# Reordered first steps of a fused FFT-mixing and ELU kernel: one weight load earlier, three reads behind the A writes, X units a step later

## The chip, the cores and the metric

The kernel runs on one core of a Trainium2 chip. The metric is the device time of one execution in microseconds (us); it was taken in three runs, and a fourth execution was recorded by the profiler. The engines are TensorE (PE for matmuls, PEld for weight loads), VectorE (DVE), ScalarE (ACT), GpSimd (POOL) and SyncE (SP), which here only issues DMA transfers. SyncE's transfers go through the DMA queue q1, GpSimd's through q0. Each engine works through its own instructions in program order; a semaphore holds an instruction back until what it reads is there.

## The reference

The input `x` has 8 batches of 3008 tokens of 256 channels. Each batch goes through a Fourier transform along its tokens, a complex linear layer with soft threshold, and the inverse transform. The result goes through two dense layers with an ELU between.

```python
X = np.fft.rfft(x, axis=1)
Yr = Xr @ w_r - Xi @ w_i + b_r
Yi = Xr @ w_i + Xi @ w_r + b_i
Yr = np.sign(Yr) * np.maximum(np.abs(Yr) - 0.01, 0.0)
Yi = np.sign(Yi) * np.maximum(np.abs(Yi) - 0.01, 0.0)
y = np.fft.irfft(Yr + 1j * Yi, n=x.shape[1], axis=1)
h = y @ moe_w_in                     # 256 -> 2048
g = np.where(h > 0.0, h, np.exp(np.minimum(h, 0.0)) - 1.0)
return g @ moe_w_out                 # 2048 -> 256
```

## The kernel before

**Two parts that run interleaved.** The transform of a batch is a chain of units, each a few matmuls with an evacuation from PSUM: six units A (first factor of the forward transform, `unit_A`), eight X (second factor, `unit_X`), twelve M (the complex layer, `unit_M`), six B (first factor of the inverse, `unit_B`) and eight Y (second factor, `unit_Y`). Between A and X, and between B and Y, the data change their layout by way of DRAM: A units write to `DA`, `load_Z` reads it back as `Z` (two pieces, rows 0 to 7 and 8 to 31 of its second axis); B units write to `DB`, and four `load_Bs` read it back as `Bs` 0 to 3. X units 0 and 1 read the first piece of Z, units 2 to 7 the second. Y units 2w and 2w+1 read `Bs` w and fill a quarter of `yT`, the input of the dense layers. `load_x` brings x of a batch in three transfers of 1 MB, on GpSimd's queue.

**Steps.** The dense layers are cut into 376 steps, 47 for each batch: step i takes a block of 512 tokens and two of the sixteen slices of 128 hidden channels. It has four matmuls into PSUM (`front_mm`, L790), exponentials on ScalarE (L804, L808), a clamp (`least`: VectorE for the first four steps, L815, then GpSimd, L813), a mix on VectorE (`mix`, L825) that gives `gT`, and two steps later eight matmuls with `w_out` (`back`, L845). Every eighth step the block's result is copied to `osb` and written to the output by four transfers (L856, L863).

**The plan.** `plan(b)` lays out what runs beside the steps of batch b: the rest of that batch's Y units and the whole chain X, M, B and the first two Y of batch b+1, and the A units of batch b+2. It makes a list `seq` with one unit for a step. `lead` is the step of the first entry, `early` says how many Y units come ahead of X, `fill` holds units that may stand among the M and B units, and `cut` says behind which M unit each of them goes (-1: ahead of the first M). `due` is the step at which the next batch's Y unit 0 stands. `f0[t]` holds the unit that is emitted between step t's two pairs of matmuls, `f1[t]` what is emitted behind them: loads, sums of weights (`weight_sum`, on GpSimd), scalings. In a step with an M unit the clamp is done by ScalarE in another form; GpSimd does four operations for each M (L274, L275, L240, L278).

**The first batch.** The transform of batch 0, the A units of batch 1 and Y units 0 and 1 of batch 0 run ahead of step 0. `w_in` is loaded in quarters on SyncE's queue (`load_w_in`) and scaled into `w_in_s` (`scale_w_in`); the last quarter's two scalings stand in steps 3 and 4 (L735), and steps 6 and 7 are the first that read it. `w_out` is loaded in halves on GpSimd's queue (`load_w_out`, L660). `gate(src)` is a copy of one element by GpSimd (L665), which waits until the transfer that brings `src` has landed; what GpSimd issues behind it starts later. There are three: ahead of x of batch 1, ahead of w_out's second half (on `Bs` 2), and in step 3 ahead of x of batch 2 (on the second piece of `Z` of batch 1).

**The order around the change.** For batch 0 `seq` is y2 to y5 in steps 1 to 4, X0 to X7 in 5 to 12, y6 in 13, M and B units from 14 on (M0, M1, M2, M3, B0, M4, M5, B1 and so on to B4 in 30), y7 in 31, B5 in 32, A0 to A3 in 33 to 36, the next batch's y0 and y1 in 37 and 38, A4 and A5 in 39 and 40. x of batch 2 is asked for in steps 3, 8 and 13. The tokens of batch 1 enter in step 40, for which its y0 and y1 are needed. Step 33 has the output writes of a block.

Of the kernel before, what the change touches and what calls it, by code (L numbers as in the profile page):

```python
# [25 lines left out]
def kernel(  # L26
# [73 lines left out]
    Z_of = {}  # L100
# [4 lines left out]
    Bs_of = {}  # L105
    yT_of = {}
    def load_x(b, ci, m0=0, m1=8):

        src = bass.AP(
            tensor=x.tensor,  # L110
            offset=x.offset + (b * S + 8 * ci + m0) * D,
            ap=[[N1 * D, N2], [(NJ - 1) * D, 2], [D, m1 - m0], [1, D]],
        )
        dst = xts[ci][:, m0:m1, :]
        nc.gpsimd.dma_start(dst, src.bitcast(F32R))
# [25 lines left out]
    def unit_A(b, u, alone=False, on_dve=False, ahead=False):  # L141
        ci, uu = u // 2, u % 2
        if uu == 0:
            if ahead and ci == 1:
                A_of[b, ci] = xtp.tile([P, 3, 8, D], BF16, name="A", tag="XT")[:, 0]
            elif ahead and ci == 2:
                A_of[b, ci] = late2.tile([P, 8, D], BF16, name="A", tag="osb")
            elif alone:
                A_of[b, ci] = wk4.tile([P, 8, D], BF16, name="A", tag="Bs")
            else:  # L150
                A_of[b, ci] = wk2.tile([P, 8, D], BF16, name="A", tag="A")
            if ci == 0:
                DA_of[b] = dram.tile([NJ, P, D], BF16, name="DA", tag="DA")
        xt, A = xts[ci], A_of[b, ci]
        dav = DA_of[b].rearrange("j p d -> p j d")
        ps = unit_ps("aps", alone or ahead)
        for j in range(2):
            nc.tensor.matmul(  # L158
                ps[:, j, :], lhsT=M1[:],
                rhs=xt[:, 4 * uu + 2 * j : 4 * uu + 2 * j + 2, :], start=True, stop=True,  # L160
            )
        def done():
            evac(
                A[:, 4 * uu : 4 * uu + 4, :].rearrange("p n d -> p (n d)"),
                ps[:].rearrange("p a b -> p (a b)"), on_dve,
            )
            j0 = 8 * ci
            if alone:
                j0 += 4 * uu
                nc.sync.dma_start(dav[:, j0 : j0 + 4, :], A[:, 4 * uu : 4 * uu + 4, :])  # L170
            elif uu == 1:
                nc.sync.dma_start(dav[:, j0 : j0 + 8, :], A[:])

        later(alone or ahead, done)
# [165 lines left out]
    def load_Bs(b, w):  # L340

        Bs = wk4.tile([4 * K1, 8, D], BF16, name="Bs", tag="Bs")
        dv = DB_of[b].rearrange("k (c h m) d -> (k c h) m d", c=2, h=2)
        nc.sync.dma_start(Bs[:], dv[:, 8 * w : 8 * w + 8, :])
        Bs_of[b, w] = Bs
# [22 lines left out]
    def idle_pe(n):  # L368

        for _ in range(n):  # L370
            nc.tensor.matmul(ips[:], lhsT=busy[:, 0:P], rhs=busy[:], start=True, stop=True)
# [278 lines left out]
    def load_w_in(q):  # L650
        if q < 3:
            wf = late3.tile([P, 2, FQ], F32, name="w_in_f", tag="Et")
        else:
            wf = late2.tile([P, 2, FQ], F32, name="w_in_f", tag="osb")
        nc.sync.dma_start(wf[:], w_in_v[:, :, q * FQ : q * FQ + FQ])
        w_in_f.append(wf)

    def load_w_out(hh):
        hf = slice(hh * NFT // 2, (hh + 1) * NFT // 2)
        nc.gpsimd.dma_start(w_out_r[:, hf, :], w_out_v[:, hf, :])  # L660

    def gate(src):

        t = gatep.tile([P, 1], F32, name="gate", tag="gate")
        nc.gpsimd.tensor_copy(t[0 : src.shape[0], :], src)  # L665
# [7 lines left out]
    for ci in range(3):  # L673
        load_x(1, ci)
    load_w_out(0)
    nc.vector.tensor_scalar(w3[:], v3[:], CMAGIC, -CMAGIC, ALU.add, ALU.add)
    nc.vector.tensor_tensor(w3[:], v3[:], w3[:], ALU.subtract)
    nc.scalar.copy(bias_p[:], brow[:])
# [53 lines left out]
    def scale_w_in(q, on_dve, c=slice(0, 2)):  # L732
        dst = w_in_s[:, c, q * FQ : q * FQ + FQ]
        if on_dve:
            nc.vector.tensor_scalar_mul(dst, w_in_f[q][:, c], 2.0 / S)  # L735
        else:
            nc.scalar.activation(dst, w_in_f[q][:, c], AF.Copy, scale=2.0 / S)

    scale_w_in(0, True)
    for u in range(6):  # L740
        unit_A(1, u, on_dve=bool(u % 2), ahead=True)
        if u == 1:
            scale_w_in(1, True)
            for w in (2, 3):
                load_Bs(0, w)
            gate(Bs_of[0, 2][:, 0, 0:1])
            load_w_out(1)
            load_w_in(3)
        idle_pe(2)
    scale_w_in(2, False)  # L750
    for s0, s1 in ((0, 8), (8, NS)):
        load_Z(1, s0, s1)
# [116 lines left out]
    def put(kind, b, *a):  # L869
        return ({"A": unit_A, "X": unit_X, "M": unit_M, "B": unit_B, "Y": unit_Y}[kind], (b, *a))  # L870

    def plan(b):

        f0 = [[] for _ in range(PER)]
        f1 = [[] for _ in range(PER)]
        n1, n2 = b + 1, b + 2
        lead = int(b == 0)
        early = 6 if b == 0 else 4
        seq = [("y", u) for u in range(2, early)]
        rest_ = []  # L880
        if n1 < B:
            due = 37 + b
            seq += [("X", u) for u in range(8)]
            fill = [("y", u) for u in range(early, 8)]
            if n2 < B:
                fill += [("A", u) for u in range(6)]
            else:
                fill += [("-",)] * 6
            room = max(0, min(10, due - 5 - (b > 0) - lead - len(seq) - 17))
            fill, rest_ = fill[:room], fill[room:]  # L890
            cut = [-1, 11, 0, 4, 8, 2, 6, 10, 1, 11][: len(fill)]
            fill = fill[::-1]
            seq += [fill.pop() for c in cut if c < 0]
            for k in range(12):
                seq.append(("M", k // 2, k % 2))
                if k % 2 and k > 1:
                    seq.append(("B", k // 2 - 1))
                for c in cut:
                    if c == k:
                        seq.append(fill.pop())  # L900
            seq.append(("B", 5))
            k = due - lead - len(seq)
            seq += rest_[:k] + [("-",)] * (k - len(rest_))
            seq += [("n", 0), ("n", 1)] + rest_[k:]
        else:
            seq += [("y", u) for u in range(early, 8)]
        xs = (3, 8, 13) if b == 0 else (1, 4, 7)
        for t, u in enumerate(seq, lead):
            if u[0] == "y":
                f0[t].append(put("Y", b, u[1]))  # L910
            elif u[0] == "n":
                f0[t].append(put("Y", n1, u[1]))
            elif u[0] == "A":
                if n2 < B:
                    f0[t].append(put("A", n2, u[1]))
            elif u[0] == "M":
                f0[t].append((unit_M, (n1, *u[1:])))
            elif u[0] != "-":
                f0[t].append(put(u[0], n1, *u[1:]))
            if u == ("X", 7):  # L920
                for k in range(2):
                    f1[t + 1].append((unit_D, (n1, k)))
            if u == ("B", 5):
                f1[t + (0 if b == 0 else 1)] += [(load_Bs, (n1, w)) for w in range(4)]
            if u == ("A", 5) and n2 < B:
                f1[t] += [(load_Z, (n2, s0, s1)) for s0, s1 in ((0, 8), (8, NS))]
        if b == 0:
            f1[5].append((weight_sum, (0,)))
            f1[6].append((weight_sum, (1,)))
            f1[7].append((weight_sum, (2,)))  # L930
            f1[3].append((scale_w_in, (3, True, 0)))
            f1[4].append((scale_w_in, (3, True, 1)))
            f1[xs[0]].append((lambda: gate(Z_of[1][:, 16, 0:1]), ()))
        if n2 < B:
            for ci in range(3):
                f1[xs[ci]].append((load_x, (n2, ci)))
        return f0, f1
# [5 lines left out]
    for i in range(n + LAG):  # L943
        split = False
        if i < n:
            r = i % PER
            if r == 0:
                f0, f1 = plan(i // PER)
                used = [bool(u0 or u1) for u0, u1 in zip(f0, f1)]
                kinds = ["M" if any(f is unit_M for f, a in f0[k]) else "F" for k in range(PER)]  # L950
# [76 lines left out]
```

## Time and profile before

| what | value |
|---|---|
| three runs | 904.35, 905.66, 907.62 us, median 905.66 |
| the profiled execution | 905.97 us |
| its span, from first to last instruction | 904.2 us |
| PE busy | 873.7 us (97%) |
| ACT busy | 709.6 us (78%) |
| POOL busy | 664.8 us (74%) |
| DVE busy | 654.7 us (72%) |
| chain of waits, shares | PE 84%, POOL 6%, issue 4%, DVE 3%, DMA 2% |
| DMA moved | 106.32 MB, mean 118 GB/s |

How to read the rows. A timeline row has start, duration, engine, line, operation, tile written and tile read, shapes and a count; merged rows cover several instructions. In square brackets stands how long the engine was idle ahead of it and what ended the idle time. The row of 40 digits is the engine's busy share in 40 slices of 22.6 us, in tenths. A row of a stage (two times with a colon) has the stage's length, the busy time and count of PE, PEld, DVE, ACT and POOL, the granted clock of TensorE as a share of full speed, the busy share of the DMA engines (it can pass 1, as transfers overlap), and the GB/s moved. Rows with SPq are SyncE's issues of transfers, not the transfers themselves; rows with POOL and DMA_DIRECT2D are GpSimd's.

### The profile page before, as it was taken

The numbers are of one execution on the slowest core, as the hardware profiler recorded it, in microseconds if no ns is written. First come the engines' busy times: TensorE is split into PE (matmuls) and PEld (weight loads), VectorE is DVE, ScalarE is ACT, GpSimd is POOL, SyncE is SP. The second block draws the span as 40 slices with busy tenths as digits, with TensorE's granted clock in tenths as the row PEclk, the third lists the DMA queues.
The fourth block names the chain that finished last, engine by engine and source line by source line (L and its number), as shares of the span: only waits on it lengthen the run. The fifth ranks groups of instructions, "written<-read, shape, count | busy, mean of one in ns | idle before, by whom it ended". The sixth has DMA issues, their size and how long they took to land.

```text
span 904.2 us, 18246 instructions
## 1 busy us (share of the span) xinstructions
PE 873.7 (97%) x6778; PEld 668.6 (74%) x6889; DVE 654.7 (72%) x1066; ACT 709.6 (78%) x1132; POOL 664.8 (74%) x998
## 2 busy tenths in 40 slices
PE   8885999999999999999999999999999999999997
PEld 3444767887778777787778877788777877778776
DVE  8772777668867687667777687767876677777775
ACT  6673888788887888888887888878887888777664
POOL 6704797669966799568986699767986589866664
PEclk9996999999999999999999999999999999999999
DMA  8995314651265411761138502573136211141011
GB/s 264 319 261 141 103 57 118 198 168 43 71 188 141 140 47 51 218 182 66 47 103 225 164 24 71 148 202 117 50 98 172 79 42 53 48 117 48 25 47 47
DMA packets 90677, 106.32 MB, mean 118 GB/s; under 512 B 5270, under 2 KB 81308, under 8 KB 87228
## 3 DMA queue, kind: packets, MB, share of 16 engines
q1 hardware_dynamic: 84332, 77.62, 30.6%
q0 software_dynamic: 5968, 27.26, 9.4%
q8 instruction: 54, 0.88, 0.4%
q14 instruction: 35, 0.29, 0.1%
q10 hardware_dynamic: 288, 0.26, 0.1%
HBM read 55.32 MB, written 49.81 MB: 116 GB/s over the span
## 4 chain that ended last, share of the span: by engine, by line
PE 84%; POOL 6%; issue 4%; DVE 3%; DMA 2%; ACT 1%; SPq 0%; ACTq 0%; DVEq 0%; POOLq 0%
PE ps_o L845 36%; PE hps L790 32%; PE mps L256 5%; PE bps L314 3%; PE xps L192 2%; PE aps L158 2%; PE yps L355 2%; POOL Y L278 1%; PE mps L209 1%; POOL yb L274 1%; POOL Et L813 1%; POOL Xd L240 1%; POOL clip L275 1%; DMA Bs<-DB 1%; DMA xt<-in_x_dram 1%
## 5 line engine op out<-in xcount | busy, mean ns | idle before, releaser
L825 DVE SCALAR_TENSOR_TENSOR gT<-Et,hps 128x512 fp32r<-128x512 f32 x752 | 496.9, 684 | 193.6 <-POOL Et L813 168.7
L845 PE MATMUL ps_o<-w_out_r,gT 128*128 128x256 f32 x3008 | 478.9, 302 | 0.9 <-ACT osb L856 0.8
L813 POOL TENSOR_SCALAR Et<-Et 128x512 f32<-128x512 f32 x576 | 351.1, 617 | 166.7 <-ACT Et L808 165.7
L845 PEld LDWEIGHTS ps_o<-w_out_r,gT 128*128 128x128 f32 x3008 | 405.2, 189 | 52.9 <-ACT osb L856 4.4
L790 PE MATMUL hps<-yT,w_in_s 128*128 128x512 bf16 (+7 forms) x1622 | 418.6, 354 | 6.2 <-DVE gT L825 4.7
L808 ACT ACTIVATE Et<-hps 128x512 f32<-128x512 f32 x584 | 341.7, 603 | 103.3 <-PE hps L790 98.9
L790 PEld LDWEIGHTS <-w_in_s 128*128 128x128 bf16 x1728 | 118.9, 98 | 61.7 <-issue 26.0
L804 ACT ACTIVATE Et<-hps 128x512 f32<-128x512 f32 x168 | 100.6, 599 | 51.9 <-PE hps L790 46.8
L278 POOL TENSOR_TENSOR Y<-yb,clip 128x512 bf16<-128x512 f32 x84 | 108.4, 1290 | 0.3
L806 ACT ACTIVATE Et<-Et 128x1024 f32<-128x1024 f32 x84 | 89.0, 1059 | 2.7
L274 POOL TENSOR_TENSOR yb<-yb,bias_d 128x256 f32<-128x256 f32 x84 | 61.6, 734 | 13.3 <-DVE yb L266 12.4
L266 DVE TENSOR_TENSOR yb<-mps,Kb 128x512 f32<-128x512 f32 x84 | 58.1, 692 | 3.0
L275 POOL TENSOR_SCALAR clip<-yb 128x512 f32<-128x512 f32 x84 | 51.7, 615 | 7.4
L240 POOL TENSOR_TENSOR Xd<-XT 128x256 bf16<-128x256 bf16 x84 | 56.3, 673 | 0.0
L265 DVE TENSOR_TENSOR Kb<-mps,bias_bc 128x256 f32<-128x256 f32 x84 | 35.5, 423 | 27.9 <-PE mps L256 27.7
L126 ACT CAST XT<-xps 128x768 bf16<-128x768 f32 x61 | 48.5, 795 | 8.9 <-PE xps L192 8.9
L126 ACT CAST A<-aps 128x1024 bf16<-128x1024 f32 x45 | 45.4, 1011 | 7.3 <-PE aps L158 6.9
L256 PE MATMUL mps<-wsum,XT 128*128 128x256 bf16 x336 | 50.4, 273 | 0.0
L126 ACT CAST yT<-yps 128x752 bf16<-128x752 f32 x63 | 49.2, 780 | 1.4 <-PE yps L355 1.4
L328 ACT CAST Bz<-bps 128x1024 bf16<-128x1024 f32 x46 | 46.3, 1007 | 0.4 <-PE bps L314 0.4
L192 PEld LDWEIGHTS <-Z 96*128 96x128 bf16 x512 | 29.2, 99 | 22.5 <-DMA Z<-DA 7.4
L192 PE MATMUL xps<-M,Z 96*128 96x96 bf16 x512 | 33.0, 208 | 9.0 <-DMA Z<-DA 6.2
(117 smaller groups left out, 476.9 us busy)
## 6 DMA issues: line engine op xcount, KB each, us to landing
xt<-in_x_dram POOLq DMA_DIRECT2D x21, 1024.0 KB, 5.3
out_dram<-osb SPq DMA_DIRECT2D x158, 128.0 KB
Bs<-DB SPq DMA_DIRECT2D x32, 384.0 KB
DA<-A SPq DMA_DIRECT2D x21, 512.0 KB
DB<-Bz SPq DMA_DIRECT2D x21, 512.0 KB
Z<-DA SPq DMA_DIRECT2D x7, 1152.0 KB
Z<-DA SPq DMA_DIRECT2D x11, 384.0 KB
xt<-in_x_dram POOLq DMA_DIRECT2D x6, 512.0 KB, 5.9
```

The costliest lines, as they stand in the source:

```text
L126: nc.scalar.copy(dst, src)
L192: nc.tensor.matmul(psv[:, kk, 0 : 4 * K1], lhsT=Z[:, k, dt * P : dt * P + P], rhs=M2[:, k].rearrange("p c m -> p (c m)"), start=True, stop ...
L256: nc.tensor.matmul(dst, lhsT=lhs(dt), rhs=rhs(dt), start=dt == 0, stop=dt == 1)
L274: nc.gpsimd.tensor_tensor(yb[:, D : 2 * D], yb[:, D : 2 * D], bias_d[:], ALU.add)
L278: nc.gpsimd.tensor_tensor(Y_[:, i, :], yb[:], clips[0][:], ALU.subtract)
L790: nc.tensor.matmul(hps[s][:, c0:c1], lhsT=w_in_s[:, dt, ft * P : ft * P + P], rhs=yT_of[b][:, dt, t0 : t0 + c1 - c0], start=(dt == 0), sto ...
L804: nc.scalar.activation(e, h, AF.Relu, scale=-1.0)
L806: nc.scalar.activation(self.E, self.E, AF.Exp, scale=-1.0)
L808: nc.scalar.activation(e, h, AF.Exp)
L813: nc.gpsimd.tensor_scalar(e, e, 1.0, 0.0, ALU.min, ALU.max)
L825: nc.vector.scalar_tensor_tensor(g_of[self.i][:, p], self.E[:, p], -1.0, self.h[p], ALU.add, ALU.max)
L845: nc.tensor.matmul(po[q][:, i_ % 2, :], lhsT=gT[:, s, i_ * P : i_ * P + P], rhs=w_out_r[:, ft, :], start=(ft == 0 and i_ % 2 == 0), stop=( ...
```

## The change

Ahead of step 0, `load_w_out(1)` is called right behind `load_w_out(0)`; the small copy that stood ahead of it is gone. `load_Bs(0, 2)`, `load_Bs(0, 3)` and `load_w_in(3)` move from behind batch 1's second A unit to behind its sixth, so that on SyncE's queue the three A writes come ahead of them, and `load_Z` behind them as before.

In the plan of batch 0 an empty entry goes in behind y3, so that y4 and y5 stand in steps 4 and 5 and the X units in 6 to 13; y6 is in 14, and the M units begin in 15. y7 goes in behind M4 (step 21) and A0 ahead of B5 (33 and 34); A1 to A3 are in 35 to 37, the next y0 and y1 in 38 and 39, A4 and A5 in 40 and 41. The two scalings of w_in's last quarter are in steps 4 and 5, x of batch 2 is asked for in steps 14, 18 and 22, and the small copy on Z ahead of it is gone.

In the plans of the later batches `due` is one larger. So one more of `fill` goes in among the M and B units, and the next batch's y0 and y1 stand a step later, in steps 38+b and 39+b; the tokens that read them enter in step 40+b.

```diff
@@ -673,6 +673,7 @@
     for ci in range(3):
         load_x(1, ci)
     load_w_out(0)
+    load_w_out(1)
     nc.vector.tensor_scalar(w3[:], v3[:], CMAGIC, -CMAGIC, ALU.add, ALU.add)
@@ -741,12 +742,10 @@
         unit_A(1, u, on_dve=bool(u % 2), ahead=True)
         if u == 1:
             scale_w_in(1, True)
-            for w in (2, 3):
-                load_Bs(0, w)
-            gate(Bs_of[0, 2][:, 0, 0:1])
-            load_w_out(1)
-            load_w_in(3)
         idle_pe(2)
+    for w in (2, 3):
+        load_Bs(0, w)
+    load_w_in(3)
     scale_w_in(2, False)
     for s0, s1 in ((0, 8), (8, NS)):
         load_Z(1, s0, s1)
@@ -877,9 +876,11 @@
         seq = [("y", u) for u in range(2, early)]
+        if b == 0:
+            seq.insert(2, ("-",))
         rest_ = []
         if n1 < B:
-            due = 37 + b
+            due = 38 + b
@@ -888,7 +889,7 @@
-            cut = [-1, 11, 0, 4, 8, 2, 6, 10, 1, 11][: len(fill)]
+            cut = ([-1, 4] if b == 0 else [-1, 11, 0, 4, 8, 2, 6, 10, 1, 11])[: len(fill)]
@@ -898,13 +899,15 @@
+            if b == 0:
+                seq.append(rest_.pop(0))
             seq.append(("B", 5))
...
-        xs = (3, 8, 13) if b == 0 else (1, 4, 7)
+        xs = (14, 18, 22) if b == 0 else (1, 4, 7)
@@ -928,9 +931,8 @@
-            f1[3].append((scale_w_in, (3, True, 0)))
-            f1[4].append((scale_w_in, (3, True, 1)))
-            f1[xs[0]].append((lambda: gate(Z_of[1][:, 16, 0:1]), ()))
+            f1[4].append((scale_w_in, (3, True, 0)))
+            f1[5].append((scale_w_in, (3, True, 1)))
```

## The prediction

> **What bounds the kernel now.** I read the page first, then the list of waits, then the timeline of 60 to 100 us, then stages of the span and SyncE's queue. On the page TensorE is busy 97% of the span; behind the first slices the only dip, down to 5 tenths, is near 70 us, and every later slice but the last shows 9.
>
> ```profile
> PE   8885999999999999999999999999999999999997
> ```
>
> The long waits of the list all lie in that dip, and the timeline shows that they are one event.
>
> ```profile
> 66.51 0.61 PE L790 MATMUL hps<-yT,w_in_s 128*128 128x512 bf16 x2
> 73.03 0.82 PE L192 MATMUL xps<-M,Z 96*128 96x96 bf16 x8 [5.91 <-DMA Z<-DA]
> ...
> 77.79 0.18 POOL L665 CAST gate<-Z 96x1 f32<-96x1 bf16 x1 [16.74 <-DMA Z<-DA]
> 78.88 1.21 POOL L813 TENSOR_SCALAR Et<-Et 128x512 f32<-128x512 f32 x2
> 79.55 1.28 DVE L825 SCALAR_TENSOR_TENSOR gT<-Et,hps 128x512 fp32r<-128x512 f32 x2 [12.35 <-POOL Et L813]
> 80.29 1.01 PE L790 MATMUL hps<-yT,w_in_s 128*128 128x512 bf16 x2 [3.88 <-DVE gT L825]
> 86.68 0.60 PE L790 MATMUL hps<-yT,w_in_s 128*128 128x512 bf16 x2
> 88.82 0.61 PE L790 MATMUL hps<-yT,w_in_s 128*128 128x512 bf16 x2
> ```
>
> Step 5 begins at 66.51; its X unit waits 5.91 us for Z's first piece, until 73.03. GpSimd's small copy waits 16.74 us for the second piece, until 77.79; behind it in GpSimd's order stands step 4's clamp (L813), behind that VectorE's mix (L825), and behind that the PSUM bank that step 6 needs: 80.29. Step 8 begins at 86.68, step 9 at 88.82. An undisturbed X step is 88.82 - 86.68 = 2.14 us. Steps 5 to 7 took 86.68 - 66.51 = 20.17 us where three such take 6.42: **13.75 us** too long.
>
> ```profile
> 66.00:68.00 2.00, 1.12 (x8) 0.59 (x7) 1.20 (x3) 1.39 (x3) 0.00 (x0) 1.00 1.37 343
> 72.00:84.00 12.00, 7.09 (x37) 5.67 (x38) 2.57 (x4) 3.40 (x5) 5.86 (x9) 0.50 0.61 170
> ```
>
> In these stages (length, then busy time of PE, PEld, DVE, ACT, POOL, then granted clock, DMA share, GB/s) the clock is 1.00 ahead of the wait and 0.50 from 72 to 84. So of the 13.75 us, 5.91 and 3.88 are waits and the other 3.96 mostly work at half clock.
>
> **Why Z is late.** SyncE issues in this order; sizes are from the DMA view.
>
> ```profile
> 51.88 0.80 SPq L344 DMA_DIRECT2D Bs<-DB  x2
> ...
> 54.94 0.95 SPq L655 DMA_DIRECT2D w_in_f<-in_moe_w_in_dram  x1
> 55.99 1.94 SPq L172 DMA_DIRECT2D DA<-A  x2
> 69.17 0.79 SPq L181 DMA_DIRECT2D Z<-DA  x2
> ...
> Bs<-DB SPq DMA_DIRECT2D x4, 384.0 KB
> DA<-A SPq DMA_DIRECT2D x3, 512.0 KB
> Z<-DA SPq DMA_DIRECT2D x1, 1152.0 KB
> w_out_r<-in_moe_w_out_dram POOLq DMA_DIRECT2D x1, 1024.0 KB, 10.0
> w_in_f<-in_moe_w_in_dram SPq DMA_DIRECT2D x1, 512.0 KB
> Z<-DA SPq DMA_DIRECT2D x1, 384.0 KB
> ...
> 52.00:54.00 2.00, 2.00 (x10) 0.85 (x9) 1.18 (x2) 1.29 (x2) 0.00 (x0) 1.00 0.52 133
> 54.00:62.00 8.00, 6.06 (x55) 3.63 (x54) 5.51 (x9) 5.51 (x10) 1.10 (x2) 1.00 1.02 293
> 70.00:76.00 6.00, 2.97 (x18) 2.61 (x18) 0.00 (x0) 1.40 (x2) 0.00 (x0) 0.59 1.02 258
> ```
>
> The last two writes of A stand behind all four Bs (1.57 MB) and w_in (0.52 MB), and in their last stretch the 1.05 MB of w_out's second half runs beside them. The DMA engines are full (share 1.02). Z is issued when the last A write has landed, at 69.17.
>
> **The change, part by part.**
>
> (1) *Order on SyncE's queue, w_out out of the way.* The new order is Bs 0 and 1 (0.79 MB), three A writes (1.57), Bs 2 and 3 (0.79), w_in (0.52), Z (0.39 and 1.18). I let the queue move in order: 0.27 MB by 54.0 (2 us at 133 GB/s), then 293 GB/s. A has landed at 54.0 + (2.36 - 0.27)/0.293 = 61.1; Bs 2, 3 and w_in are through at 61.1 + 1.31/0.293 = 65.6; Z, at its own 258 GB/s, at 67.1 and 71.7. From the last byte to use I add 1.7 us: the old Z's 1.57 MB, at 258 from 70.0 on, ends at 76.1, and the copy that waits for it runs at 77.79. Usable: Bs 2 at 64.1, w_in at 67.3, Z at **68.8** and **73.4**. Needed: y4 stays in step 4, which begins a step ahead of 66.51, so 0.45 us later, at 64.8 (0.45 for the two matmuls ahead of a unit); X0 is now in step 6, at 66.51 + 2.14 + 0.45 = **69.1**, X2 two steps on at **73.4**. That leaves 0.7, 0.3 and 0.0 us. I take 0.3 us for the waits left; bounds are 0, and 3.4 by the first rival below. If the waits go, all 13.75 us go, since the half clock came with them.
>
> (2) *scale_w_in a step later.* The second scale now stands in step 5, directly ahead of step 6, whose matmuls read it.
>
> ```profile
> 66.78 0.42 DVE L735 TENSOR_SCALAR w_in_s<-w_in_f 128x512 bf16<-128x512 f32 x1
> ```
>
> The old one ended at 67.20, 0.69 us behind the front of the following step (66.51), which did not need it. The new one does the same a step later, and there it is needed: **+0.7 us**. With w_in usable at 67.3, 0.5 us behind the place of the new first scale (66.78), the bounds are 0 and 1.2.
>
> (3) *w_out's second half at 28 us.* It is issued in an idle gap of GpSimd's.
>
> ```profile
> 27.13 1.28 POOL L660 DMA_DIRECT2D w_out_r<-in_moe_w_out_dram  x1
> 32.92 1.24 POOL L300 TENSOR_SCALAR clip<-yb 128x512 f32<-128x512 f32 x1 [4.50 <-DVE yb L219]
> DMA to landing us min/median/max: 10.0/12.0/13.9
> 40.00:46.00 6.00, 5.95 (x44) 2.53 (x43) 3.41 (x5) 5.31 (x8) 4.19 (x6) 1.00 0.53 175
> ```
>
> The issue ends at about 29.7, ahead of the clip at 32.92: nothing. The first half landed at 27.13 + 13.9 = 41.0, so the second moves from 40 to 46, where 6 x 0.175 = 1.05 MB move now. At the 343 GB/s that w_out and SyncE's queue reached together (66 to 68 us), 2.06 MB would fit, 0.04 less than needed; at 293, 0.34 less. What is left over could delay the last DB write, and with it Bs 0, by 0.1 or 1.2 us; that write is issued only behind 49 us, so I take **+0.2**, bounds 0 and 1.2. *The Trainium skill, "DMA: Bandwidth & Descriptors", section "Queues, rings and completion order", speaks against this edit: a DMA engine goes round robin between the queues that have work, packet by packet, so w_out would take about half of each engine from the DB writes while both run. By that rule every DB write of this stage could end late by w_out's own 3.1 us (1.05 MB at 343 GB/s), but those issued ahead of 46 us have no reader before 51; the sum stays.*
>
> (4) *X units a step later, y7 among the M steps, x of batch 2 at steps 14, 18, 22, no small copies.* Steps and units stay in number, so TensorE's own time stays. What counts is GpSimd's work in the M steps of batch 0.
>
> ```profile
> 99.55 0.61 PE L790 MATMUL hps<-yT,w_in_s 128*128 128x512 bf16 x2
> 102.02 0.39 PE L790 MATMUL hps<-yT,w_in_s 128*128 128x512 bf16 x1
> 144.14 0.61 PE L790 MATMUL hps<-yT,w_in_s 128*128 128x512 bf16 x2
> 99.61 0.58 POOL L115 DMA_DIRECT2D xt<-in_x_dram  x1
> ```
>
> The 17 steps (12 M, 5 B) from 99.55 to 144.14 took 44.59 us; at the first one's 2.47 they would take 41.99, so 2.6 us are lost, to GpSimd, which the chain of waits follows through most of this stretch. The new order puts y7 among them, a step with 1.21 us of clamps in 2.14: 0.93 us relieved. Two x issues (0.58 each, steps 18 and 22) come in: 1.16. **+0.2 us**, bounds -0.9 and +1.2. The issue at 99.61 stood there before, too.
>
> (5) *y of batch 1 four steps behind that batch's last B, not five; step 33's four output writes now ahead of that B's write on SyncE.*
>
> ```profile
> 151.77 1.74 SPq L344 DMA_DIRECT2D Bs<-DB  x4
> 153.60 2.68 SPq L863 DMA_DIRECT2D out_dram<-osb  x4
> 158.38 0.50 PE L355 MATMUL yps<-M,Bs 96*128 96x94 bf16 x8
> 55.54 0.84 PE L355 MATMUL yps<-M,Bs 96*128 96x94 bf16 x16 [0.62 <-DMA Bs<-DB]
> ```
>
> From the first Bs issue to its use was 55.54 - 51.88 = 3.66 us, so here Bs was ready at 155.4 and needed at 158.4: 3.0 us in hand. One step less takes 2.1 to 2.5. The outputs' 2.68 us of issue begin as their block ends, and I estimate that 0.7 us of them stand ahead of the B write; their 0.52 MB may hold the rings for 1.8 us (at 293). So the wait lies between 0 and about 2: **+0.6 us**.
>
> (6) *Later batches: one more unit among the M steps, y of the next batch a step later.* The page's row shows TensorE at 9 tenths or more through all of them, so an M step is not shortened by what stands beside it: 0, bounds -0.5 and +0.5 as estimates from the 2.6 us of batch 0. The second y unit now ends in the step right ahead of its first reader.
>
> ```profile
> 269.71 0.78 ACT L126 CAST yT<-yps 128x752 bf16<-128x752 f32 x1
> 270.71 1.04 PE L790 MATMUL hps<-yT,w_in_s 128*128 128x512 bf16 x4
> ```
>
> Its cast ends at 270.49 and the next step begins at 270.71: covered, by 0.2 us.
>
> **Sum.** -13.75 + 0.3 + 0.7 + 0.2 + 0.2 + 0.6 = -11.75. The profiled execution took 905.97 us (span 904.2 and 1.8 around it), which becomes 894.2; it lies 0.3 above the median of the three runs, 905.66, which becomes **893.9**.
>
> **Rivals.**
>
> *Z is still late.* For it: three margins in (1) are 0.7 us or less. If the queue moves at Z's 258 GB/s throughout, and Bs and w_in share it with the A writes, A lands at 54.0 + 3.40/0.258 = 67.2; Z is issued 0.9 later and begins 0.9 behind that, as the old one did (69.17 to about 70), so it is usable at 72.2 and 76.8: 3.1 us of wait at X0 and 0.3 at X2, 3.1 more than taken: **897.0**. Against it: the queue moved 293 with both kinds on it. *By the Trainium skill, "TensorE: Matmul & The Clock Gate", part on the HAM clock gate, the clock halves behind an idle window of about 3.4 us; the trace agrees so far as a wait of 5.9 us was followed by 0.50. By that rule a wait of 3.1 just escapes it, and one of 3.5 costs up to 3.96 more, as here: 901.*
>
> *GpSimd becomes the bound at once.* Its three weight sums lay in the disturbed steps and cost nothing there; now they lie in X steps at full speed.
>
> ```profile
> 80.05 1.16 POOL L228 TENSOR_TENSOR wsum<-wcat_r 128x512 bf16<-128x512 bf16 x1
> ```
>
> If three of at most 1.16 us and the two x issues all come onto the path, it is 3.5 + 1.2 - 0.2 = 4.5 more: **898.4**. Against it: two clamps are 1.21 of a step's 2.14, so a sum fits but for 0.2.
>
> *Slower: GpSimd is held at the issue of w_out's second half.* No row shows five transfers of 1 MB in its queue at once. Were it held until the queue is empty, 41.0 + 3.1 = 44.1, the clip of 32.92 would be 11.2 us late, TensorE would idle behind it and go on at half clock for another 3.96 as above: +15.2, **909.1**. From a hold to about 41 us on (8.1 + 3.96 = 12.1), nothing of the gain is left. Against it: four went in one behind the other.
>
> *It does not do what it says*: A still lands near 69 us because something else than the order holds it. Then Z's wait stays, less the step that X has moved: near 903. No row speaks for it.
>
> **How the numbers follow.** The forecast holds 0.65; its own range, from the bounds taken together, is 891 to 896. Z still late 0.17, GpSimd 0.1, held 0.05, no effect 0.03. The range, 890.8 to 898.5, takes in the prices of the first two rivals. A change under 0.3%, 2.7 us, cannot be told from none: faster than 902.9 are the first three, 0.92; same 0.03; slower 0.05.
>
> **What would show it.** Right: no copy on Z in GpSimd's order, Z issued near 62, X0 at 69 to 70, clock 1.00 from 60 to 100. A scale of w_in that ends behind the front of step 6 shows (2); a wait of TensorE for Bs in step 38 shows (5); M steps of batch 0 that keep 2 to 3 us of loss show (4). Wrong would be a GpSimd issue of several us at 28, Z issued behind 66, or a clock below 1.00 after 60.

## The result and the profile after

| kernel | median | lowest to highest | runs | ratio to the kernel before, with its 95% interval |
|---|---|---|---|---|
| before | 905.66 us | 904.35 to 909.50 | 19 | |
| changed | 903.20 us | 901.19 to 905.58 | 19 | 0.9973 [0.9963, 0.9982] |

The change is worth 2.5 us where 11.75 were forecast, and the time lies outside the range. The profiled execution took 905.58 us, 0.4 less than that of before (905.97). It is the slowest of the nineteen, 2.4 us above their median, so its profile can show losses that most executions do not have. Most of the expected gain was made, and most of it was lost again 600 us later. The page shows both in the row of TensorE's slices of the kernel after.

```profile
PE   8888999999999999999999999999997999999997
```

The dip to 5 near 70 us is gone, but there is a new one, down to 7, in the 31st slice (22.6 us each, so from 678 to 701 us).

**The first steps: 10.0 us won.** SyncE's issues in the kernel after, and then TensorE's timeline; the columns are those of before.

```profile
52.09 0.80 SPq L344 DMA_DIRECT2D Bs<-DB  x2
52.98 1.00 SPq L172 DMA_DIRECT2D DA<-A  x2
55.15 2.36 SPq L172 DMA_DIRECT2D DA<-A  x1
57.56 2.43 SPq L344 DMA_DIRECT2D Bs<-DB  x2
60.04 0.46 SPq L655 DMA_DIRECT2D w_in_f<-in_moe_w_in_dram  x1
61.96 0.78 SPq L181 DMA_DIRECT2D Z<-DA  x2
```

```profile
56.27 0.84 PE L355 MATMUL yps<-M,Bs 96*128 96x94 bf16 x16 [1.36 <-DMA Bs<-DB]
...
67.71 0.39 PE L789 MATMUL hps<-yT,w_in_s 128*128 128x512 bf16 x1
...
72.60 0.39 PE L789 MATMUL hps<-yT,w_in_s 128*128 128x512 bf16 x1 [1.48 <-DVE w_in_s L736]
72.83 0.51 PE L192 MATMUL xps<-M,Z 96*128 96x96 bf16 x8
...
74.53 0.61 PE L789 MATMUL hps<-yT,w_in_s 128*128 128x512 bf16 x2
...
76.68 0.61 PE L789 MATMUL hps<-yT,w_in_s 128*128 128x512 bf16 x2
```

Z is issued at 61.96 where it was 69.17, and X0, at 72.83, waits for nothing. Step 8 begins at 76.68 where it was 86.68. What is missing from the 13.75 us: y0 comes at 56.27 where it was 55.54 (0.73); steps 0 to 2 ran partly at half clock and took 0.8 us more (6.12 where it was 5.33; below); steps 5 and 6 together, from 67.71 to 74.53, took 6.82 us where 4.28 is undisturbed: 2.5 us for the last quarter of w_in. The step without a unit, at 1.80 us, gave 0.3 back, but only for a while, since the unit that it leaves out runs later. VectorE's scalings of it, and GpSimd in the same stretch:

```profile
69.06 1.04 DVE L736 TENSOR_SCALAR w_in_s<-w_in_f 128x512 bf16<-128x512 f32 x1 [1.25 <-DMA w_in_f<-in_moe_w_in_dram]
...
71.22 1.33 DVE L736 TENSOR_SCALAR w_in_s<-w_in_f 128x512 bf16<-128x512 f32 x1
```

```profile
68.66 1.16 POOL L228 TENSOR_TENSOR wsum<-wcat_r 128x512 bf16<-128x512 bf16 x1
...
71.12 1.14 POOL L228 TENSOR_TENSOR wsum<-wcat_r 128x512 bf16<-128x512 bf16 x1
```

w_in is late (issued at 60.04, usable at 69.06), and a scaling that took 0.42 us before takes 1.04 and 1.33 while a weight sum runs. The clamps of steps 5 and 6 are queued behind those sums, the mixes behind the scalings. Not every execution has this: due5_back, z7_behind_bs and outs_behind (below) have the same first steps, and in their profiles w_in came in time and steps 5 and 6 took 4.4 us. In that of due_old_all it was late again, and they took 8.34, partly at a clock of 0.57.

**Batch 5's last steps: 7.5 us lost.** TensorE in the kernel after, around 690 us, and then a stage behind the wait with its clock.

```profile
687.89 1.04 PE L789 MATMUL hps<-yT,w_in_s 128*128 128x512 bf16 x3
...
689.69 0.61 PE L789 MATMUL hps<-yT,w_in_s 128*128 128x512 bf16 x2
695.50 0.81 PE L355 MATMUL yps<-M,Bs 96*128 96x94 bf16 x8 [5.21 <-DMA Bs<-DB]
...
698.67 1.08 PE L789 MATMUL hps<-yT,w_in_s 128*128 128x512 bf16 x2
...
705.55 0.50 PE L355 MATMUL yps<-M,Bs 96*128 96x94 bf16 x8
```

```profile
696.00:700.00 4.00, 4.00 (x22) 2.99 (x21) 0.69 (x1) 1.60 (x3) 0.61 (x1) 0.50 0.89 269
```

Of the kernel before, TensorE at the same two places:

```profile
695.80 0.60 PE L790 MATMUL hps<-yT,w_in_s 128*128 128x512 bf16 x2
...
705.96 0.41 PE L355 MATMUL yps<-M,Bs 96*128 96x94 bf16 x6
```

Step 42 of batch 5 begins at 687.89 where it was 695.80, a lead of 7.9 us. The first y unit among batch 6's own steps is at 705.55 where it was 705.96: the lead is 0.4. In between, step 43 holds y0 of batch 6; it began at 689.69 and took 8.98 us, since TensorE stood 5.21 us for Bs and went on at a clock of 0.50. The next step took 2.79. That is 6.84 + 0.65 = 7.5 us over 2.14 each.

Why Bs was late is on SyncE. First the kernel after, then the kernel before:

```profile
678.14 0.37 SPq L172 DMA_DIRECT2D DA<-A  x1
681.41 0.80 SPq L181 DMA_DIRECT2D Z<-DA  x2
682.30 0.38 SPq L336 DMA_DIRECT2D DB<-Bz  x1
691.25 1.71 SPq L344 DMA_DIRECT2D Bs<-DB  x4
```

```profile
686.06 0.37 SPq L336 DMA_DIRECT2D DB<-Bz  x1
688.47 0.36 SPq L172 DMA_DIRECT2D DA<-A  x1
689.31 2.28 SPq L344 DMA_DIRECT2D Bs<-DB  x4
691.97 1.04 SPq L181 DMA_DIRECT2D Z<-DA  x2
```

The order is turned round. In batch 5's plan the later `due` lets one more unit in among the M and B units, and the last A unit moves from step 37 to step 36, ahead of B5, which moves from 36 to 37. Behind the last A write stands the load of Z (1.57 MB) for batch 7, whose first reader runs at 709.84; B5's write of 0.52 MB is now queued behind it. The chain of waits of the kernel after names both halves of the delay:

```profile
682.30 8.93 DMA DB<-Bz
...
691.25 4.21 DMA Bs<-DB
```

From B5's write to the issue of Bs it took 8.95 us, where it was 689.31 - 686.06 = 3.25: 5.7 us more. In those 8.95 us 2.11 MB moved, at 236 GB/s: Z's 1.57, B5's 0.52 and hardly anything else.

### The profile page after: what moved, and what is told of

It reads as the page before. It is cut to its first block, busy times and chain, and to the rows that moved or that the text cites. A ratio compares the mean times of both kernels' runs of the same rounds, so it can differ in the third digit from the quotient of the medians.

```text
span 903.8 us, 18245 instructions
## 1 busy us (share of the span) xinstructions
PE 875.0 (97%) x6779; PEld 668.0 (74%) x6889; DVE 655.4 (73%) x1066; ACT 709.3 (78%) x1132; POOL 663.8 (73%) x996
## 4 chain that ended last, share of the span: by engine, by line
PE 84%; DMA 5%; POOL 4%; DVE 3%; ACT 2%; issue 2%; SPq 1%; ACTq 0%; DVEq 0%; POOLq 0%
PE ps_o L844 36%; PE hps L789 31%; PE mps L256 6%; PE bps L314 3%; PE aps L158 2%; PE xps L192 2%; PE yps L355 2%; PE mps L209 1%; DMA w_in_f<-in_moe_w_in_dram 1%; DMA DB<-Bz 1%; POOL Y L278 1%; DMA DA<-A 1%; DMA xt<-in_x_dram 1%; POOL yb L274 1%; POOL Et L812 1%
## 5 line engine op out<-in xcount | busy, mean ns | idle before, releaser
L355 PEld LDWEIGHTS <-Bs 96*128 96x128 bf16 x512 | 28.9, 100 | 22.2 <-DMA Bs<-DB 8.4
L355 PE MATMUL yps<-M,Bs 96*128 96x94 bf16 x512 | 32.7, 210 | 8.1 <-DMA Bs<-DB 7.0
```

Source lines behind the costliest of these rows:

```text
L355: nc.tensor.matmul(psv[:, j, 0 : 2 * N1], lhsT=Bs[:, j, dt * P : dt * P + P], rhs=M4[:], start=True, stop=True,)
```

## The experiments

The theory after this comparison: the first steps gained nearly what was forecast, and the loss is the place of Z's load in batch 5 on SyncE's queue. The rivals: the loss comes from the new order of units itself, or the small copy on Z is all that mattered in the first steps. All kernels were timed in five rounds against the kernel before, with medians from 905.58 to 905.91 for it. A microsecond or so between two kernels with four to six runs each is within the spread of their runs.

| kernel | starts from | median | range | runs | ratio [95%] |
|---|---|---|---|---|---|
| z7_behind_bs | changed | 896.26 | 895.50 to 898.23 | 4 | 0.9897 [0.9884, 0.9911] |
| due5_back | changed | 896.57 | 895.27 to 899.85 | 5 | 0.9899 [0.9881, 0.9916] |
| before_due | before | 913.80 | 913.20 to 914.56 | 4 | 1.0088 [1.0074, 1.0102] |
| gate_only | before | 904.14 | 901.55 to 904.78 | 11 | 0.9975 [0.9966, 0.9984] |
| w_out_only | before | 903.43 | 902.26 to 906.71 | 12 | 0.9975 [0.9964, 0.9987] |
| due_old_all | due5_back | 897.86 | 894.92 to 899.05 | 6 | 0.9907 [0.9891, 0.9922] |
| w_out_late | due5_back | 904.37 | 902.52 to 908.33 | 12 | 0.9986 [0.9973, 0.9998] |
| old_order | due5_back | 896.31 | 895.88 to 897.71 | 4 | 0.9898 [0.9883, 0.9913] |
| x2_early | due5_back | 897.77 | 896.19 to 898.88 | 5 | 0.9908 [0.9894, 0.9923] |
| outs_behind | due5_back | 895.20 | 893.80 to 896.66 | 4 | 0.9888 [0.9870, 0.9907] |
| sums_later | due5_back | 895.16 | 894.17 to 896.83 | 4 | 0.9885 [0.9869, 0.9901] |
| all_three | due5_back | 894.66 | 893.11 to 895.11 | 4 | 0.9871 [0.9854, 0.9889] |

### Z's load of batch 7 three steps later

```diff
-                f1[t] += [(load_Z, (n2, s0, s1)) for s0, s1 in ((0, 8), (8, NS))]
+                f1[t + (3 if b == 5 else 0)] += [(load_Z, (n2, s0, s1)) for s0, s1 in ((0, 8), (8, NS))]
```

> Edit to the changed kernel: in the plan of batch 5 alone, the loads of batch 7's Z are emitted three steps later (step 39), so that on SyncE's queue they stand behind batch 6's last B write and the loads of its Bs; every unit keeps its step. Theory 1 (order on SyncE's queue): the 7.5 us lost at batch 6's first y units (steps of 8.98 and 2.79 where 2.14 is usual) come from 1.57 MB of Z standing ahead of that write; they all come back: 903.2 - 7.5 = 895.7 us. Rival (unit order): Bs is late because the last B unit itself stands in step 37 instead of 36, close to a block's output writes; then this edit gives back nothing: 903.

Measured: 896.26 us, 6.9 less than the changed kernel. Every unit keeps its step. SyncE's issues, and TensorE at step 43:

```profile
680.69 0.36 SPq L336 DMA_DIRECT2D DB<-Bz  x1
683.92 1.74 SPq L344 DMA_DIRECT2D Bs<-DB  x4
...
689.40 1.93 SPq L181 DMA_DIRECT2D Z<-DA  x2
```

```profile
690.37 0.50 PE L355 MATMUL yps<-M,Bs 96*128 96x94 bf16 x8
```

B5's write to the issue of Bs is 3.2 us again, and y runs at 690.37 with no wait. The write is issued 1.6 us earlier, too: in the changed kernel it stood behind Z's issue, which waited for the last A write. So the cause is the queue's order, and not the order of the units.

### Batch 5's due step as it was

```diff
-            due = 38 + b
+            due = 38 + b - (b == 5)
```

> Edit to the changed kernel: due stays at its old value in the plan of batch 5 alone, so that there the last B unit again stands in step 36 and the last A unit in 37, ahead of their transfers in that order. Theory 1 (order of the transfers) and the unit-order rival both expect about 895.7 us here; a third one, that the loss seen in one profile isn't that of most runs (the changed kernel's runs spread over 4.4 us), expects 903 or a gain of 2 to 3 us at most.

Measured: 896.57 us, 6.6 less, the same from the other side: with B5 ahead of A5 again, the loss is gone. This kernel is the base of the later experiments.

### Only the later due step, on the kernel before

```diff
-            due = 37 + b
+            due = 37 + b + (b > 0)
```

> Edit to the kernel before: due is one larger in the plans of batches 1 to 6, and nothing else is changed. Theory 1: the later batches' part alone costs the 7.5 us of batch 5's swap: 905.7 + 7.5 = 913.2 us. The prediction's own step (6), that the later batches cost nothing, expects 905.7, from 905.2 to 906.2.

Measured: 913.80 us, 8.0 slower than before. SyncE and TensorE of this kernel:

```profile
689.92 0.80 SPq L181 DMA_DIRECT2D Z<-DA  x2
690.82 0.38 SPq L336 DMA_DIRECT2D DB<-Bz  x1
699.79 1.71 SPq L344 DMA_DIRECT2D Bs<-DB  x4
```

```profile
703.68 0.81 PE L355 MATMUL yps<-M,Bs 96*128 96x94 bf16 x8 [4.87 <-DMA Bs<-DB]
```

The whole pattern appears without any edit of the first steps. By itself this part of the change is a plain loss.

### The old due step in all later batches

```diff
-            due = 38 + b - (b == 5)
+            due = 37 + b + (b == 0)
```

> Edit to the changed kernel: due keeps its old value in the plans of all later batches, and its new one in batch 0's alone. Theory 1 (the swap of two loads in batch 5's plan is the whole cost of the later batches' part): as due5_back, 896.6 us within 0.7. Rival (the extra filler and the later y units of batches 1 to 4 and 6 cost or gain something too): off by more than 1 us.

Measured: 897.86 us, with an interval that overlaps that of due5_back. Outside batch 5 the later step is worth nothing that these runs can tell.

### Only the small copy on Z taken away, on the kernel before

```diff
-            f1[xs[0]].append((lambda: gate(Z_of[1][:, 16, 0:1]), ()))
```

> Edit to the kernel before: the small copy on Z ahead of x of batch 2 is left out, and nothing else is changed. Theory 2 (two waits in a row): the wait for Z's first piece stays, the 3.88 us behind the copy and a part of the half clock go: 900 to 901.5 us. Rival (shared queues): x of batch 2, 1 MB, now starts at about 67 us beside Z's 1.57 MB and makes Z later by up to 3 us for each piece, so that the wait moves from GpSimd to the X units: 904 to 906.

Measured: 904.14 us, 1.7 less than before. GpSimd's issue of x and TensorE's X0:

```profile
61.62 0.67 POOL L115 DMA_DIRECT2D xt<-in_x_dram  x1
```

```profile
76.00 0.82 PE L192 MATMUL xps<-M,Z 96*128 96x96 bf16 x8 [8.30 <-DMA Z<-DA]
```

GpSimd is free, but TensorE now waits 8.30 us for Z where it was 5.91: x of batch 2 is asked for at 61.62, ahead of Z, and shares the engines with what Z waits for and then with Z: from Z's issue, at 68.50, to X0 it took 7.5 us, where it was 3.9. The wait went from GpSimd to X0. So the copy cost little on balance: it held GpSimd, and it kept x of batch 2 from Z.

### Only w_out early, on the kernel before

```diff
+    load_w_out(1)
...
-            gate(Bs_of[0, 2][:, 0, 0:1])
-            load_w_out(1)
```

> Edit to the kernel before: w_out's second half is asked for right behind the first, and the small copy on Bs that stood ahead of it is gone; all else as before (order of the A writes, copy on Z, X in step 5). Theory 5 (w_out beside the A writes made them late): Z is issued at about 66 us instead of 69.2, both old waits get 3 us shorter, the clock may stay full: 899 to 902. Rival (w_out cost nothing there): 905.9.

Measured: 903.43 us, 2.2 less. The copy on Z still holds GpSimd, for longer than before since no other copy stands ahead of it:

```profile
74.84 0.18 POOL L665 CAST gate<-Z 96x1 f32<-96x1 bf16 x1 [30.26 <-DMA Z<-DA]
```

It runs at 74.84 where it was 77.79. Z came about 3 us earlier, as expected: X0 waited 2.57 us where it was 5.91. But the wait behind the copy grew from 3.88 to 4.46, again at about half clock, so the time stayed above the 899 to 902 expected. Neither the copy's removal nor the early w_out has the gain alone.

### w_out late again

```diff
-    load_w_out(1)
...
+    gate(Bs_of[0, 2][:, 0, 0:1])
+    load_w_out(1)
```

The two added lines stand behind batch 1's A units. 

> Edit to due5_back: w_out's second half is again asked for late, behind batch 1's A units and a small copy on Bs 2, instead of at 28 us. Theory 3 (w_out beside Z is one of the causes of the old wait): its 1.05 MB at about 63 us runs beside w_in and Z and makes both 2 to 3 us later, TensorE waits about 2 us at step 6: 898 to 900. Rival (the order of the A writes alone does it): 896.6, or up to 1 us better, as the DB writes and Bs 0 no longer share the engines with w_out.

Measured: 904.37 us, 7.8 more than due5_back. The size says that w_out matters, but the place was another than expected: X0 ran at 69.54, and the wait came behind it.

```profile
69.54 0.51 PE L192 MATMUL xps<-M,Z 96*128 96x96 bf16 x8
...
76.51 2.07 PE L845 MATMUL ps_o<-w_out_r,gT 128*128 128x256 f32 x8 [6.03 <-DMA w_out_r<-in_moe_w_out_dram]
```

TensorE stood 6.03 us for w_out itself: its second half, which GpSimd issued at 63.72 behind the copy, is read from step 6 on. In the kernel before, that half landed at 70.1 (60.07 and 10.0 us), and step 6, held by Z, read it at 82.2; undisturbed it would have read it near 70, by an estimate from 66.51, a step of 2.14 and the 1.0 from a step's front to these matmuls. Z's wait had hidden that w_out was barely in time.

### The old order of the A writes

```diff
         if u == 1:
             scale_w_in(1, True)
+            for w in (2, 3):
+                load_Bs(0, w)
+            load_w_in(3)
         idle_pe(2)
-    for w in (2, 3):
-        load_Bs(0, w)
-    load_w_in(3)
```

> Edit to due5_back: Bs 2, Bs 3 and w_in's last quarter go back ahead of batch 1's later A writes on SyncE's queue; w_out stays early, the small copies stay out, X stays in step 6. If the order of the A writes is the main part of the gain (prediction's step 1): Z is issued at about 66 us, 4 us later, TensorE waits 1 to 3.4 us at step 6 and may fall to half clock: 898 to 902. Rival (w_out out of the way, the missing copy and the later X step are enough): 896.6 to 897.2.

Measured: 896.31 us, the same as due5_back. Z is issued later than in the changed kernel, at 66.01, and X2 waits for it a little.

```profile
66.01 0.79 SPq L181 DMA_DIRECT2D Z<-DA  x2
```

```profile
74.70 0.51 PE L192 MATMUL xps<-M,Z 96*128 96x96 bf16 x8 [0.34 <-DMA Z<-DA]
```

X2's step took 2.67 us, 0.5 too long. In return w_in, issued at 54.9 in this order, is not late. With w_out out of the way and X a step later, the place of the A writes is not what decides.

### x of batch 2 early, without the copy

```diff
-        xs = (14, 18, 22) if b == 0 else (1, 4, 7)
+        xs = (3, 8, 13) if b == 0 else (1, 4, 7)
```

> Edit to due5_back: x of batch 2 is asked for in steps 3, 8 and 13 again, without the small copy. Theory 2 (x beside Z makes Z late, as in gate_only, where X0 waited 8.3 us instead of 5.9): Z's pieces come 2 to 3 us later, TensorE waits as long at step 6 or 8: 898 to 900. Rival (Z has room enough now): 896.6, or less, as two issues leave GpSimd's M steps.

Measured: 897.77 us, 1.2 more than due5_back, with overlapping intervals. Z is not late: X0 runs at 72.98 without a wait. What stands out is ahead of it. GpSimd's issue, and TensorE's y0:

```profile
49.88 0.64 POOL L115 DMA_DIRECT2D xt<-in_x_dram  x1 [5.14 <-PE aps L158]
```

```profile
58.36 1.43 PE L355 MATMUL yps<-M,Bs 96*128 96x94 bf16 x16 [3.58 <-DMA Bs<-DB]
```

GpSimd has nothing to do in steps 0 to 3, so an issue that is put down for step 3 goes out as soon as its buffer is free, at 49.88. It runs beside the first Bs, and y0 comes at 58.36, later than in any other profile. But without this edit y0 lay anywhere from 55.14 to 57.80, so one profile does not show that x is the cause, and the runs do not show a loss.

### The output writes of step 33 two steps later

```diff
-                        (nc.scalar if last and i_ % 2 == 0 else nc.sync).dma_start(
-                            ov[w, r0 : r0 + k // 8], osb[c0 : c0 + k, i_, :]
-                        )
+                        send = (nc.scalar if last and i_ % 2 == 0 else nc.sync).dma_start
+                        args = (ov[w, r0 : r0 + k // 8], osb[c0 : c0 + k, i_, :])
+                        if i == 31:
+                            put_off.append((send, args))
+                        else:
+                            send(*args)
...
+            if i == 35:
+                for send, args in put_off:
+                    send(*args)
```

> Edit to due5_back (the changed kernel with the old due in batch 5's plan, 896.6 us): the four output writes of step 33 are issued in step 35, behind batch 1's last B write and its Bs loads; copies and units keep their places. Prediction's step (5) (outputs ahead of the B write make Bs late for the y unit in step 38): the wait there, 1.26 us in due5_back's profile, and the 0.5 us at A5 behind it go: 894.8, from 894 to 895.6. Rival (four steps are too few whatever stands on the queue, 3.2 us of landing and 3.66 from issue to use): no change, 896.6.

Measured: 895.20 us, 1.4 less than due5_back in the medians, with overlapping intervals, so the gain is not shown; the trace shows what became of the wait. First the changed kernel, then this one, at the first y of batch 1 (step 38):

```profile
151.32 0.51 PE L355 MATMUL yps<-M,Bs 96*128 96x94 bf16 x8 [0.39 <-DMA Bs<-DB]
...
158.55 0.73 PE L158 MATMUL aps<-xt,M 128*128 128x512 f32 x2 [0.48 <-ACT A L126]
```

```profile
147.03 0.50 PE L355 MATMUL yps<-M,Bs 96*128 96x94 bf16 x8
```

With the outputs behind B's write the wait for Bs is gone. In due5_back's profile that wait was 1.08 us. The changed kernel's second row is its last A unit, which waits for the cast of the A unit ahead of it; that cast waited 1.08 us for an earlier A write. This step stays long here, with 2.82 us against 3.04. Of the 2.8 us between the profiled executions of due5_back and this kernel, 1.8 lie ahead of step 8, where the two do not differ.

### The weight sums four steps later

```diff
-            f1[5].append((weight_sum, (0,)))
-            f1[6].append((weight_sum, (1,)))
-            f1[7].append((weight_sum, (2,)))
+            f1[9].append((weight_sum, (0,)))
+            f1[10].append((weight_sum, (1,)))
+            f1[11].append((weight_sum, (2,)))
```

> Edit to due5_back: the three weight sums on GpSimd move from steps 5, 6, 7 to 9, 10, 11. Theory 4 (VectorE and GpSimd get in each other's way): the scalings of w_in in steps 4 and 5 take 0.42 us in every profile instead of 0.77 to 1.33 where a sum runs beside them, and step 6 loses its 0.1 to 1.6 us: 895.8, from 895 to 896.5. Rival (the scale is long since its input is late or by chance): its length stays above 0.7, 896.6.

Measured: 895.16 us, 1.4 less than due5_back in the medians; the intervals overlap, so the time alone does not settle it. VectorE's scalings in this kernel, then the second one of due5_back, and the front of step 8 in this kernel:

```profile
66.35 0.43 DVE L736 TENSOR_SCALAR w_in_s<-w_in_f 128x512 bf16<-128x512 f32 x1
...
67.89 0.58 DVE L736 TENSOR_SCALAR w_in_s<-w_in_f 128x512 bf16<-128x512 f32 x1
```

```profile
69.76 0.77 DVE L736 TENSOR_SCALAR w_in_s<-w_in_f 128x512 bf16<-128x512 f32 x1
```

```profile
72.69 0.60 PE L789 MATMUL hps<-yT,w_in_s 128*128 128x512 bf16 x2
```

The scalings take 0.43 and 0.58 us, and w_in is not waited for in this execution. Step 8 begins 14.0 us ahead of the kernel before, 0.3 of it through the step without a unit: the whole of the 13.75 can be had. The sums' place gave little of that. Due5_back's step 8 began 2.0 us later; 1.9 of these lie in steps 0 to 2 and ahead of them, where y0 came later and the clock fell, and 0.1 in steps 3 to 7. The later sums are a guard for executions in which w_in is late: in all_three it was waited for, 0.65 us, and steps 5 and 6 took 4.79 us, not 6.82 or 8.34.

### The three together

The edits of due5_back, outs_behind and sums_later in one kernel.

> The three edits together on the changed kernel: old due in batch 5's plan, step 33's output writes behind the B write and its Bs loads, weight sums in steps 9 to 11. If the gains of the last two (1.4 us each in their medians) are separate causes, they add: 896.6 - 2.8 = 893.8 us. If the weight sums' 1.4 was the spread of the runs (its profile shows 0.1 us at step 6), 895.2.

Measured: 894.66 us, the shortest median of all, 10.9 us less than before and 8.5 less than the changed kernel. It is less than the sum of the single medians would give: beside outs_behind (895.20) the later sums are worth half a microsecond at most, and four runs of each don't show even that. Its page:

```profile
PE   8889999999999999999999999999999999999997
```

No slice of TensorE behind the first three shows less than 9 until the last, and the dip at 690 us is gone.

## Why the prediction was wrong, and where it was right

**The step that failed is (6), "later batches: 0".** It looked at two things that a moved unit touches, TensorE's pace and the cast of y, and the runs show no loss from these (due_old_all against due5_back). It did not follow the transfers that the moved A unit issues. Its write and the load of Z behind it passed B5's write on SyncE's queue, and y, which needs that write, had only 10 us in hand (686.06 to 696.24 before). The price was 7.5 us, 8.0 by itself on the kernel before; the bound given was 0.5. The quantity was at hand before the result: `seq` of batch 5 can be written out from the kernel's `plan`, and the DMA view has Z's size. Step (5) asked this very question of batch 0, where the outputs pass the B write, and (6) did not ask it again.

With that one swap undone the kernel takes 896.3 to 896.6 us, inside the range, 2.4 to 2.7 above the forecast. The other steps:

(1) *Z in time*: right in its result. Z was issued at 61.96, as forecast near 62, and X0 and X2 waited for no Z. The reason was wrong in part. With the copy out and X a step later, either of the two other edits was enough for X0: it did not wait in w_out_late, with the A writes first, nor in old_order, with w_out early. X2 waited 0.34 us in old_order; in w_out_late it stands behind the wait for w_out and can't tell. W_out had to come early for its own sake, since step 6 reads it.

(2) *scale_w_in a step later*: mechanism right, size off: 2.5 us in the profiled execution where 0.7 was taken, bounds 0 and 1.2. w_in was issued only at 60.04, since SyncE spent 2.36 us on the third A issue and 2.43 on two of Bs (that the full DMA engines held these issues is likely, but not shown), and was usable at 69.06 instead of 67.3. And the scaling ran beside a weight sum. Where w_in came in time the price was 0.1 (due5_back, z7_behind_bs, outs_behind), less than the 0.7: the size of this term depends on the execution. The rival on GpSimd counted the sums as time on GpSimd, not as a brake on VectorE.

(3) *w_out at 28 us*: the first Bs are issued at 52.09 where it was 51.88, 0.2 us as taken, and no issue of GpSimd's held the clips. But y0 came 0.73 later than before, and half clock at 58 to 62 us was in no step: together 1.5 us in the profiled execution. This varies between executions: up to y0 due_old_all and z7_behind_bs are the same program, and y0 came at 55.14 and 57.80; sums_later's profile has neither loss.

(4) *M steps of batch 0*: right in the sum; its two parts were not told apart. They run from 91.70 to 138.67 (46.97 us), where TensorE's own pace makes 44.13 (17 steps at 2.47 and y7's 2.14): 2.8 us are lost, 0.2 more than before.

(5) *y of batch 1, and the outputs ahead of B's write*: right in place and cause, as outs_behind shows; step 38 took 0.56 us too long (2.70 against 2.14) where 0.6 was taken, and 1.26 in due5_back's profile. The last A unit's step, 3.04 us where 2.31 is usual, adds 0.7 that was in no step.

The sum over the profiled execution closes: forecast 894.2; 2.5 more in the first steps (10.0 won instead of 12.55), 0.7 more at step 41, and 7.5 in batch 5 make 904.9, and 905.58 was measured. Of the remaining 0.7, 0.3 is the unit that step 3 leaves out and that runs later, and 0.2 goes between step 42 of batch 0 (160.51 where it was 168.65, a lead of 8.1) and batch 5 (7.9); the rest was not traced.

Two more points on the prediction. Its own range, 891 to 896, does not follow from its bounds: added up without the first rival's 3.4 they give 890.5 to 898.3. And two of its signs pointed to trouble in the first steps: X0 came at 72.83, not at 69 to 70, and the clock was 0.57 from 60 to 62 us. It had no sign for batch 5.

Of the rivals none was what happened. "Z still late" and "GpSimd held" did not come. "It does not do what it says" gave nearly the right time, near 903, for a wrong reason: Z did come early. A transfer that a moved unit brings ahead of an urgent one was not among them.

## What to carry to other kernels

A unit that is moved takes its transfers with it: write out the new order of every queue, for every batch in which the plan comes out differently, and compare the bytes ahead of each urgent write with the time its reader has in hand. A plan made by a rule (here `due` and the room it leaves) can swap two units in one batch only, and an average over batches does not show it. When a wait goes, ask what it had hidden: here w_out, which was itself barely in time.

## What the runs showed of the hardware

**A VectorE scaling is held by a GpSimd sum.** Alone it takes 0.42 us (the kernel before). Beside the two sums that run from 68.66 to 69.82 and from 71.12 to 72.26 it ends at 70.10 and 72.55, both times 0.3 us behind the end of the sum. The Trainium skill, "SBUF — State Buffer", section "SBUF: two separate sides", says that VectorE and GpSimd share a pair of memory ports, and that a VectorE operation in a two-port mode and a GpSimd operation exclude each other on it: the one that starts first keeps the pair for its whole length. The ends of the two scalings fit a block; that this scaling runs in a two-port mode no run here shows. With the sums moved away the scalings took 0.43 and 0.58, and beside one sum the second took 0.77 in due5_back, again ending 0.3 us behind the sum.

**TensorE's clock falls to about half behind some short waits, and not behind others.** Idle time ahead of y0 and the granted clock in the stage of 58 to 62 us, by kernel:

| kernel | idle ahead of y0, us | clock |
|---|---|---|
| due_old_all | 0.52 | 1.00 |
| before | 0.62 | 1.00 |
| old_order | 0.91 | 0.57 |
| outs_behind | 0.98 | 1.00 |
| changed | 1.36 | 0.57 |
| w_out_only | 1.38 | 1.00 |
| due5_back | 1.62 | 0.59 |
| x2_early | 3.58 | 0.50 |

From 0.9 to 1.4 us it goes both ways. The other kernels fit: 0.49, 0.77, 0.85 and 1.28 us left the clock at 1.00 (sums_later, w_out_late, all_three, gate_only), 1.42 gave 0.57 (before_due), and 2.87 gave 0.77 (z7_behind_bs, whose y0 ran only at 57.80). Where the clock fell, steps 0 to 2 together took 0.6 to 0.9 us more (5.86 in due5_back and 6.12 in the changed kernel, 5.22 in sums_later), which may be part of the spread between runs. The Trainium skill, "TensorE: Matmul & The Clock Gate", part on the HAM clock gate, which the prediction used, has the clock fall behind an idle window of about 3.4 us; here waits well under that were followed by half clock, so the length of this one wait doesn't decide it. What does was not found.

**A write behind a long transfer on the same queue waited for it.** The same 0.52 MB took 3.2 us from issue to the next issue that needs it with nothing large ahead (z7_behind_bs), and 8.95 behind 1.57 MB, the time in which both moved.
